# An MoE stage that is activated in place in PSUM, with its queues in written order

## The chip, the core and the metric

One core of a Trainium2 chip runs the whole program. The metric is device time in microseconds (us) of one execution. The core has five engines that this document speaks of: TensorE (PE) multiplies matrices into PSUM, eight banks of 512 fp32 columns on 128 partitions; VectorE (DVE) and ScalarE (ACT) read and write both PSUM and SBUF; GpSimd (POOL) works on SBUF alone; SyncE (SP) issues the DMAs. Each engine takes its instructions strictly in the order of its own queue, so an instruction that waits holds up all behind it.

## What is computed

Attention with a cluster mask over 2 x 8 heads, then two MoE-like layers on 1536 tokens of width 512 (2048 hidden). Only the two layers are touched:

```python
x = attn_out.transpose(0, 2, 1, 3).reshape(1536, 512)
h = x @ w_in;  g = maximum(0.01 * h, h);  x = g @ w_out        # layer one
h = x @ w2_in; r = maximum(h, 0); g = r * r; out = g @ w2_out   # layer two
```

Everything is fp32 in and out. TensorE gets each operand as a high and a low part in a reduced format (`xh`, `xl`, `wh`, `wl`, `gh`, `gl`), and each product is three matmuls: high by high, high by low, low by high.

## The kernel before

**Layers.** A layer is eight pairs of 128-wide slices f of the hidden dimension. Tokens are three blocks b of 512. A unit (`g1`) is h of one b and one f: four 128-deep chunks times three, 12 matmuls of 128x512 into one PSUM bank. It is activated (`act`) to `gh` and `gl` in SBUF; then `g2` multiplies them with the second weight, 12 matmuls over four banks `o`, which are open over the two f of a pair. After a pair, `flush` moves the four banks: into `acc` by ACT for the first pair (L839), added to it by DVE for the others (L842), and for the last pair added (L846), then split to `xh` (ACT, L847) and `xl` (DVE and POOL in turn, L848) as the next layer's input.

**Plain pairs and quads.** The first `PLAIN[m]` pairs of layer m are plain: six units. The others are quads: blocks 0 and 1 and both f are taken together by seven products in place of eight (`quad`), 42 matmuls in place of 48, and block 2 by two units. The quad needs sums of rows of x (`t_pieces`: `whole` at L896 on DVE joins high and low part, `minus` on POOL at L904, and `keep` splits the result into `th` on ACT and `tl` on DVE and POOL at L909), one overwritten part of x (`t_last`, L932 and L933), and a third weight block of sums (`sum_pieces`, POOL, L190). All of the x sums are written into the last plain pair, f = 2. Block 2's two `g2` stand in the next pair ("behind").

**Weights.** A slice's weight block is loaded as 8-byte floats (1 MB, `wraw`, one buffer, L140, SP queue) and made fp32: `mag` on ACT (L149), `shift`, `low`, `sign` on DVE (L153, L159, L166), then split: `wh` on ACT (L128), `wl` on POOL (L129). The next load can start only when `sign` has read the raw words. The pieces are laid evenly between the steps of the pair before.

**Activation.** Layer one: ACT applies Prelu twice to the bank, once to `gh`, once to an SBUF tile `g` (L795, L796), and `gl` is their difference (L803), on DVE for units, on POOL inside a quad. Layer two: ACT writes Relu to an SBUF tile `t` (L799), DVE squares it to `g` (L800), ACT rounds to `gh` (L801), then `gl`. Inside a quad the pieces are first added from a bank and an SBUF tile to another SBUF tile `q` (L871, L884, L888).

**What sets the order.** The attention stage is written out by hand. From `manual.close()` (L718), near attention's end, a planner that works with estimated durations orders PE, DVE, ACT and POOL; it takes the `ps_h` pool's four banks in turn and mixes matmuls of several units. SP's queue is in written order, and so is PE's last step.

Of the kernel before, what the change touches and what calls it, by code (L numbers as in the profile page):

```python
# [52 lines left out]
def attention_moe_moe_kernel(  # L53
# [69 lines left out]
    def split_block(ci, t):  # L123
        pool = next(q for q, n in ring if ci % RING < n)
        wh = pool.tile([128, 2 * DM], F32R, tag="wh", name="wh")
        wl = pool.tile([128, 2 * DM], F32R, tag="wl", name="wl")
        weights[blocks[ci]] = (wh, wl)
        nc.scalar.copy(out=wh, in_=t)  # L128
        nc.gpsimd.tensor_tensor(out=wl, in0=t, in1=wh.bitcast(F32), op=ALU.subtract)  # L129

    def decode_pieces(ci):

# [35 lines left out]
                op0=ALU.bitwise_and, op1=ALU.bitwise_or,  # L168
            )

        def split():
            split_block(ci, st["t"].bitcast(F32))

        return [load, mag, shift, low, sign, split]

    def sum_pieces(ci):

        st = {}
        K = DM // 2

        def sums():
            w = st["w"] = stg[1].tile([128, 4, K], F32, tag="ws", name="ws")
            t0, t1 = words.pop(ci - 2), words.pop(ci - 1)
            for o, i, k, op in (
                (w[:, 0], t1[:, 0:K], t1[:, K : 2 * K], ALU.add),
                (w[:, 1], w[:, 0], t0[:, 0:K], ALU.subtract),
                (w[:, 2], t0[:, 0:K], t1[:, 0:K], ALU.subtract),
                (w[:, 3], t0[:, K : 2 * K], w[:, 1], ALU.subtract),
            ):
                nc.gpsimd.tensor_tensor(out=o, in0=i, in1=k, op=op)  # L190

        def split():
            split_block(ci, st["w"].rearrange("p a b -> p (a b)"))

        return [sums, split]

    def pool_copy(out, in_):
        nc.gpsimd.tensor_scalar(
# [574 lines left out]
    def x_in(kk, b):  # L773
        return tuple(x[:, kk, b * N : (b + 1) * N] for x in (xh, xl))
# [61 lines left out]
    def flush(m, b, g, o, ps):  # L836
# [19 lines left out]

    def quad(m, f, between):
# [6 lines left out]
        U = ps_h.tile([128, N], F32, tag="h", name="h")  # L864
        p(U, lambda k: w_in(f0, k), lambda k: x_in(k, 0), True)
        p1 = tmp()
        nc.scalar.copy(out=p1, in_=U)
        V = ps_h.tile([128, N], F32, tag="h", name="h")
        p(V, lambda k: w_in(f0, 2 + k), lambda k: x_in(2 + k, 0), True)
        h = tmp()  # L870
        nc.vector.tensor_tensor(out=h, in0=V, in1=p1, op=ALU.add)  # L871
        act(m, 0, f, h, True)
        between(0)
        p(U, lambda k: w_in(s, 2 + k), lambda k: t_in(1, k), False)
        u2 = tmp()
        nc.scalar.copy(out=u2, in_=U)
        W = ps_h.tile([128, N], F32, tag="h", name="h")
        p(W, lambda k: w_in(s, k), lambda k: t_in(0, k), True)
        p5 = tmp()
        nc.scalar.copy(out=p5, in_=W)  # L880
        between(1)
        p(U, lambda k: w_in(s, 4 + k), lambda k: t_in(2, k), False)
        h = tmp()
        nc.vector.tensor_tensor(out=h, in0=U, in1=p5, op=ALU.add)  # L884
        act(m, 1, f + 1, h, True)
        p(W, lambda k: w_in(s, 6 + k), lambda k: x_in(2 + k, 1), False)
        h = tmp()
        nc.vector.tensor_tensor(out=h, in0=W, in1=u2, op=ALU.add)  # L888
        act(m, 1, f, h, True)
        p(U, lambda k: w_in(f1, 2 + k), lambda k: t_in(3, k), False)  # L890
        act(m, 0, f + 1, U)

    def whole(k, b):
        h, l = x_in(k, b)
# [2 lines left out]
        return t  # L897

    def t_pieces(kk):
        st = {}  # L900

        def minus(x, y, *tag):
            t = tmp(*tag)
            nc.gpsimd.tensor_tensor(out=t, in0=x, in1=y, op=ALU.subtract)  # L904
            return t

        def keep(i, t):
            nc.scalar.copy(out=th[:, i, kk], in_=t)
            (nc.vector if i % 2 else nc.gpsimd).tensor_tensor(  # L909
                out=tl[:, i, kk], in0=t, in1=th[:, i, kk].bitcast(F32), op=ALU.subtract  # L910
            )

        def first():
            st["b12"] = whole(kk, 1)
            st["t"] = minus(st["b12"], whole(kk, 0))
            keep(0, st["t"])

        def second():
            st["b22"] = whole(2 + kk, 1)
            st["t"] = minus(st["b22"], st["t"])  # L920
            keep(1, st["t"])

        def third():
            keep(2, minus(st["b22"], st["b12"]))
            t_late[kk] = minus(whole(2 + kk, 0), st["t"], "t4", 2)

        return [first, second, third]
# [9 lines left out]
    def step_list(m, f, prev):  # L937
# [9 lines left out]
        if f < 2 * PLAIN[m]:  # L947
# [5 lines left out]
            if f == 2 * PLAIN[m] - 2:  # L953
                t = t_pieces(0) + t_pieces(1)
                seq = [g for p in zip(seq, t) for g in p] + seq[len(t) :]
                seq += [lambda: (t_last(0), t_last(1))]
# [12 lines left out]
    for m in range(2):
        for f in range(0, NF, 2):  # L970
            seq, prev = step_list(m, f, prev)
            after = (m, f + 2) if f + 2 < NF else (m + 1, 0)
            pcs = []
            for i, block in enumerate(blocks):
                if block[:2] == after:
                    pcs += (sum_pieces if block[2] == 2 else decode_pieces)(i)
            done = 0
            for i, step in enumerate(seq):
                if (m, f, i) == (1, NF - 2, len(seq) - 1):
                    with tc.manual_schedule(engines={mybir.EngineType.PE}):  # L980
                        step()
                else:
                    step()
                if (m, f, i) == (0, 0, 0):
                    for pc in decode_pieces(1):
                        pc()
                upto = len(pcs) * (i + 1) // len(seq)
                for pc in pcs[done:upto]:
                    pc()
                done = upto  # L990
# [47 lines left out]
```

## Time and profile before

| | us |
|---|---|
| median of the runs (3: 793.75 to 794.24) | 794.1 |
| the profiled execution | 793.11 |
| its span, first to last instruction | 791.3 |
| PE busy in the span | 758.3 |
| DVE busy | 619.5 |
| POOL busy | 451.8 |
| ACT busy | 443.9 |

A stretch is read from the busy time of PE, the number of its instructions and the granted clock there. An instruction's row gives its start, its duration, what it makes of what, and, in brackets, how long its engine had been idle before it and who released it. PE's matmuls overlap, so the pace is read from starts, not from durations.

### The profile page before, as it was taken

The numbers are of one execution on the slowest core, as the hardware profiler recorded it, in microseconds if no ns is written. First come the engines' busy times: TensorE is split into PE (matmuls) and PEld (weight loads), VectorE is DVE, ScalarE is ACT, GpSimd is POOL, SyncE is SP. The second block draws the span as 40 slices with busy tenths as digits, with TensorE's granted clock in tenths as the row PEclk, the third lists the DMA queues.
The fourth block names the chain that finished last, engine by engine and source line by source line (L and its number), as shares of the span: only waits on it lengthen the run. The fifth ranks groups of instructions, "written<-read, shape, count | busy, mean of one in ns | idle before, by whom it ended". The sixth has DMA issues, their size and how long they took to land.

```text
span 791.3 us, 11086 instructions
## 1 busy us (share of the span) xinstructions
PE 758.3 (96%) x4075; PEld 655.6 (83%) x4075; DVE 619.5 (78%) x838; ACT 443.9 (56%) x823; POOL 451.8 (57%) x372
## 2 busy tenths in 40 slices
PE   8899999999999898989999999989799999999998
PEld 8899999999988776868887888866588888888886
DVE  5899999999998987664776773899787687877654
ACT  6988988988997455344253452545443444344420
POOL 2989889888863874445354441687543435273410
PEclk9999999999999998999999999999999999999999
DMA  7584474463403122320330221111311102111004
GB/s 221 121 204 108 111 170 118 109 154 92 123 1 108 54 80 80 106 88 20 106 107 1 77 86 51 53 54 54 101 60 59 48 22 86 54 54 53 1 1 159
DMA packets 16006, 66.35 MB, mean 84 GB/s; under 512 B 2704, under 2 KB 2704, under 8 KB 10960
## 3 DMA queue, kind: packets, MB, share of 16 engines
q1 hardware_dynamic: 15952, 65.64, 28.2%
q8 instruction: 32, 0.52, 0.3%
q14 instruction: 22, 0.18, 0.1%
HBM read 44.60 MB, written 3.15 MB: 60 GB/s over the span
## 4 chain that ended last, share of the span: by engine, by line
PE 62%; DVE 24%; ACT 6%; issue 3%; DMA 3%; POOL 2%; DVEq 0%; ACTq 0%; POOLq 0%; SPq 0%
PE o L826 26%; PE h L764 21%; PE S L386 4%; PE A L484 4%; DVE el L466 4%; PE T L449 4%; DVE nm L409 4%; DMA wraw<-w 3%; DVE q L896 2%; ACT e L419 2%; DVE wt L159 2%; DVE wt L166 2%; DVE gl L803 2%; DVE wt L153 2%; POOL ws L190 1%
## 5 line engine op out<-in xcount | busy, mean ns | idle before, releaser
L842 DVE TENSOR_TENSOR acc<-o,acc 128x512 f32<-128x512 f32 x144 | 95.0, 685 | 51.8 <-PE o L826 51.7
L803 POOL TENSOR_TENSOR gl<-g,gh 128x512 fp32r<-128x512 f32 x36 | 52.4, 1462 | 125.7 <-ACT gh L801 71.2
L129 POOL TENSOR_TENSOR wl<-wt,wh 128x1024 fp32r<-128x1024 f32 x32 | 81.1, 2535 | 61.4 <-ACT wh L128 61.2
L764 PE MATMUL h<-xl,wh 128*128 128x512 f32 x288 | 112.4, 390 | 0.6 <-DVE xl L848 0.6
L764 PE MATMUL h<-xh,wh 128*128 128x512 f32 x288 | 112.0, 391 | 0.0
L764 PE MATMUL h<-xh,wl 128*128 128x512 f32 x288 | 110.8, 390 | 0.0
L436 POOL TENSOR_SCALAR e<-e,r 128x768 f32<-128x768 f32 x96 | 88.5, 932 | 21.5 <-DVE r L433 14.2
L466 DVE TENSOR_TENSOR el<-T,eh 128x512 fp32r<-128x512 f32 x144 | 94.3, 683 | 5.8 <-ACT eh L460 3.9
L409 DVE TENSOR_REDUCE nm<-S 128x1 f32<-128x768 f32 x96 | 90.7, 946 | 4.1 <-PE S L290 2.3
L419 ACT ACTIVATE e<-S,nm 128x768 f32<-128x768 f32 x96 | 87.0, 907 | 11.0 <-DVE nm L409 6.7
L386 PE MATMUL S<-hb 128*128 128x384 f32 (+1 forms) x384 | 90.6, 350 | 1.9 <-ACT e L419 1.2
L460 ACT CAST eh<-T 128x512 fp32r<-128x512 f32 x144 | 79.4, 586 | 11.9 <-PE T L449 11.4
L826 PE MATMUL o<-wh,gh 128*128 128x512 f32 x192 | 76.6, 399 | 8.0 <-ACT acc L839 5.3
L484 PE MATMUL A<-eh,vv 128*128 128x256 f32 x288 | 79.5, 306 | 2.6 <-DVE xt L506 2.6
L449 PE MATMUL T<-ident,e 128*128 128x128 f32 x576 | 79.7, 274 | 1.2 <-DVE el L466 1.0
L826 PE MATMUL o<-gl,wh 128*128 128x512 f32 x192 | 76.7, 399 | 3.8 <-DVE gl L803 3.8
L826 PE MATMUL o<-gh,wh 128*128 128x512 f32 x192 | 73.1, 399 | 6.1 <-ACT acc L839 3.1
L826 PE MATMUL o<-wl,gh 128*128 128x512 f32 x192 | 75.8, 395 | 0.0
L826 PE MATMUL o<-gh,wl 128*128 128x512 f32 x192 | 75.7, 396 | 0.0
L826 PE MATMUL o<-wh,gl 128*128 128x512 f32 x192 | 73.1, 396 | 1.8 <-DVE gl L803 1.8
L484 PE MATMUL A<-el,vv 128*128 128x256 f32 x288 | 72.5, 282 | 0.3 <-DVE el L466 0.3
L449 PEld LDWEIGHTS T<-ident,e 128*128 128x128 f32 x576 | 68.3, 144 | 5.2 <-POOL e L436 1.7
(136 smaller groups left out, 1694.3 us busy)
## 6 DMA issues: line engine op xcount, KB each, us to landing
wraw<-w SPq DMA_DIRECT2D x32, 1024.0 KB, 4.7
hb<-spl SPq DMA_DIRECT2D x14, 576.0 KB, 4.7
hb<-spl SPq DMA_DIRECT2D x42, 192.0 KB, 4.9
rqk<-qk SPq DMA_DIRECT2D x16, 384.0 KB, 4.2
rv<-v SPq DMA_DIRECT2D x8, 384.0 KB, 4.0
out<-q SPq DMA_DIRECT2D x12, 256.0 KB, 2.0
twice<-qk SPq DMA_DIRECT2D x8, 192.0 KB, 5.9
hb<-st SPq DMA_DIRECT2D x28, 48.0 KB, 2.6
```

Of the source, the lines that this page charges most:

```text
L129: nc.gpsimd.tensor_tensor(out=wl, in0=t, in1=wh.bitcast(F32), op=ALU.subtract)
L386: nc.tensor.matmul(out=s[:, c, 0:HALF], lhsT=hb[0:k, a, i * 128 : (i + 1) * 128], rhs=hb[0:k, b, c * HALF : (c + 1) * HALF], start=(a == 0 ...
L409: nc.vector.tensor_reduce(out=n, in_=s_t[t][:, :, 0:HALF], axis=AX.XY, op=ALU.max, negate=True)
L419: nc.scalar.activation(out=e.rearrange("p (a b) -> p a b", a=2), in_=s_t.pop(t)[:, :, 0:HALF], func=AF.Exp, bias=n_t.pop(t), scale=1.0, ac ...
L436: nc.gpsimd.tensor_scalar(out=e_t[t], in0=e_t[t], scalar1=r_t[t // 2][:, t % 2 : t % 2 + 1], scalar2=1.0, op0=ALU.mult, op1=ALU.mult,)
L449: nc.tensor.transpose(T[:, o : o + 128], e_t[2 * u + b][:, kc * 128 : (kc + 1) * 128], ident)
L460: nc.scalar.copy(out=eh[:, 2 * g : 2 * g + 2, :].rearrange("p a b -> p (a b)"), in_=T_t[u, g])
L466: nc.vector.tensor_tensor(out=el[:, 2 * g : 2 * g + 2, :].rearrange("p a b -> p (a b)"), in0=T_t.pop((u, g)), in1=eh[:, 2 * g : 2 * g + 2, ...
L484: nc.tensor.matmul(out=A, lhsT=w, rhs=m[:, kc, :], start=(kc == 0 and i == 0), stop=(kc == KC - 1 and i == 1),)
L764: nc.tensor.matmul(out=out, lhsT=l, rhs=r, start=(first and i == 0), stop=(i == n - 1), skip_group_check=not first,)
L826: nc.tensor.matmul(out=outs[o], lhsT=l, rhs=r, start=(first and i == 0), stop=(last and i == 2),)
L842: nc.vector.tensor_tensor(out=a, in0=ps, in1=a, op=ALU.add)
```

## The change

In layer one the first three pairs are plain (two before); layer two keeps two. `act` works in the unit's own bank: the second Prelu, the square and the quad's three additions write back to PSUM, the square as max(h, 0) times Relu's tile in one DVE instruction, and `gl` is always DVE's, also in quads. The four `ps_h` banks are taken by name: U, V, W, X in a quad, fixed ones for units. The steps of a quad become three (`first`, `second`, `third`), and inside `third` the activation's parts of three units are interleaved by hand. From the second pair of layer one, (m, f) = (0, 2), to the end PE, DVE, ACT and POOL run in written order; the first pair stays with the planner. A table `TURN` says after which step of a pair each piece of the next pair's weights stands (0 load, 1 mag, 2 shift, 3 low, 4 sign, 5 `wh`, 6 `wl`; block 2: sums, `wh`, `wl`; block "3" is the load for the pair after next). The x sums are cut into eight pieces a chunk, one after each step from `SUMS`, so over pairs two and three of layer one and over the first two pairs of layer two; `minus` and all of `tl` and `xl` are POOL's, `whole` stays DVE's.

```diff
-    PLAIN = (2, 2)
+    PLAIN = (3, 2)
...
-        nc.gpsimd.tensor_tensor(out=wl, in0=t, in1=wh.bitcast(F32), op=ALU.subtract)
+        return lambda: nc.gpsimd.tensor_tensor(
+            out=wl, in0=t, in1=wh.bitcast(F32), op=ALU.subtract
+        )
...
-    ps_h = ctx.enter_context(tc.tile_pool(name="ps_h", bufs=4, space=PSUM, reuse_waits="tile"))
+    ps_h = ctx.enter_context(tc.tile_pool(name="ps_h", bufs=1, space=PSUM, reuse_waits="tile"))
...
-        h = ps_h.tile([128, N], F32, tag="h", name="h")
+        h = bank((2 * b + f + f // 2 * 2) % 4 if f < 2 * PLAIN[m] else (1, 3)[f % 2])
...
+        def relu():
             nc.scalar.activation(out=t, in_=h, func=AF.Relu)
-            nc.vector.tensor_tensor(out=g, in0=t, in1=t, op=ALU.mult)
-            nc.scalar.copy(out=gh, in_=g)
-        eng = nc.gpsimd if inside else nc.vector
-        eng.tensor_tensor(out=gl, in0=g, in1=gh.bitcast(F32), op=ALU.subtract)
-        parts[m, b, f] = gh, gl
+
+        def square():
+            nc.vector.scalar_tensor_tensor(
+                out=h, in0=h, scalar=0.0, in1=t, op0=ALU.max, op1=ALU.mult
+            )
+
+        def high():
+            if m == 0:
+                nc.scalar.activation(out=gh, in_=h, func=AF.Prelu, alpha=0.01)
+                nc.scalar.activation(out=h, in_=h, func=AF.Prelu, alpha=0.01)
+            else:
+                nc.scalar.copy(out=gh, in_=h)
+
+        def low():
+            nc.vector.tensor_tensor(out=gl, in0=h, in1=gh.bitcast(F32), op=ALU.subtract)
+            parts[m, b, f] = gh, gl
...
-            (nc.vector if o % 2 else nc.gpsimd).tensor_tensor(
+            nc.gpsimd.tensor_tensor(
                 out=xl[:, o, c], in0=a, in1=xh[:, o, c].bitcast(F32), op=ALU.subtract
             )
...
+        U, V, W, X = (bank(i) for i in range(4))
+
+        def first():
+            p(U, lambda k: w_in(f0, k), lambda k: x_in(k, 0), True)
+            p1 = tmp()
+            nc.scalar.copy(out=p1, in_=U)
+            p(V, lambda k: w_in(f0, 2 + k), lambda k: x_in(2 + k, 0), True)
+            add(V, V, p1)
+            act(m, 0, f, V)
...
+        def third():
+            u2, p5 = kept
+            p(U, lambda k: w_in(s, 4 + k), lambda k: t_in(2, k), False)
+            add(X, U, p5)
+            x = acts(m, 1, f + 1, X)
+            w = acts(m, 1, f, W)
+            u = acts(m, 0, f + 1, U)
...
+        return [
+            lambda: (whole("b12", kk, 1), whole("b11", kk, 0)),
+            lambda: (minus("t1", "b12", "b11"), whole("b22", 2 + kk, 1)),
+            lambda: (minus("t2", "b22", "t1"), high(0, "t1")),
+            lambda: (low(0, "t1"), high(1, "t2")),
+            lambda: (minus("t3", "b22", "b12"), whole("b21", 2 + kk, 0)),
+            lambda: (low(1, "t2"), high(2, "t3")),
+            lambda: (minus("t4", "b21", "t2", "t4", 2), t_late.update({kk: st["t4"]})),
+            lambda: low(2, "t3"),
+        ]
...
-            lambda: quad(m, f, lambda i: i < len(behind) and behind[i]()),
+            first, behind[0], second, behind[1], third,
             out_of(0, 0), unit(2, 0), out_of(0, 1), unit(2, 1), out_of(1, 0), out_of(1, 1),
...
+    TURN = (
+        ((0, 1),), ((0, 2), (0, 3)), ((0, 4), (1, 0)), ((0, 5),), ((0, 6), (1, 1)),
+        ((1, 2), (1, 3)), ((1, 4), (2, 0)), ((1, 5), (1, 6), (3, 0)), ((2, 1),), ((2, 2),),
+    )
+    SUMS = ((11, 22), (3, 11))
+    LAST = (30, 19)
```

ACT at the end of attention, where layer one's first pair begins (`T` and `A` are attention's banks, `h_3736` is the first unit's bank, `wh` and `wt` the weight block for the second pair), before:

```order
L497 COPY xt_3483<-A_3654 64x256
L460 CAST eh_3660<-T_3681 128x512
L149 ACTIVATE wt_3788<-wraw_3767 128x1024
L497 COPY xt_3483<-A_3687 64x256
L795 ACTIVATE gh_3750<-h_3736 128x512
L796 ACTIVATE g_3749<-h_3736 128x512
L795 ACTIVATE gh_3783<-h_3769 128x512
L796 ACTIVATE g_3782<-h_3769 128x512
L128 CAST wh_3847<-wt_3788 128x1024
```

and with the change:

```order
L151 ACTIVATE wt_3768<-wraw_3766 128x1024
L499 COPY xt_3483<-A_3654 64x256
L462 CAST eh_3660<-T_3681 128x512
L128 CAST wh_3827<-wt_3768 128x1024
L499 COPY xt_3483<-A_3687 64x256
L811 ACTIVATE gh_3749<-h_3736 128x512
L812 ACTIVATE h_3736<-h_3736 128x512
L811 ACTIVATE gh_3783<-h_3770 128x512
```

The weight block's `wh` now stands ahead of attention's last copy and of the first unit's activation; it stood behind both. On PE the second unit and part of two others moved ahead of attention's last product `A_3687`, and right behind that product stand now the first `g2`'s matmuls.

DVE in layer two's first pair (`q` from `xh`,`xl` are the x sums, `acc` from `o` is the flush of layer one), before:

```order
L848 TENSOR_TENSOR xl_67<-acc_3733,xh_66 128x512
L800 TENSOR_TENSOR g_5773<-t_5776 128x512
L153 TENSOR_SCALAR wt_6019<-wt_6019 128x1024
L896 TENSOR_TENSOR q_6075<-xh_66,xl_67 128x512
L846 TENSOR_TENSOR acc_3733<-o_5726,acc_3733 128x512
L159 SCALAR_TENSOR_TENSOR wt_6019<-wraw_6001,wt_6019 128x1024
L800 TENSOR_TENSOR g_5796<-t_5799 128x512
L803 TENSOR_TENSOR gl_5775<-g_5773,gh_5774 128x512
L909 TENSOR_TENSOR tl_3735<-q_6023,th_3734 128x512
L896 TENSOR_TENSOR q_6077<-xh_66,xl_67 128x512
L848 TENSOR_TENSOR xl_67<-acc_3733,xh_66 128x512
```

and with the change:

```order
L866 TENSOR_TENSOR acc_3733<-o_5664,acc_3733 128x512
L805 SCALAR_TENSOR_TENSOR h_5692<-h_5692,t_5707 128x512
L817 TENSOR_TENSOR gl_5706<-h_5692,gh_5705 128x512
L805 SCALAR_TENSOR_TENSOR h_5714<-h_5714,t_5729 128x512
L817 TENSOR_TENSOR gl_5728<-h_5714,gh_5727 128x512
L155 TENSOR_SCALAR wt_5712<-wt_5712 128x1024
L161 SCALAR_TENSOR_TENSOR wt_5712<-wraw_5592,wt_5712 128x1024
L805 SCALAR_TENSOR_TENSOR h_5736<-h_5736,t_5751 128x512
L817 TENSOR_TENSOR gl_5750<-h_5736,gh_5749 128x512
L168 SCALAR_TENSOR_TENSOR wt_5712<-wraw_5592,wt_5712 128x1024
L959 TENSOR_TENSOR q_5778<-xh_66,xl_67 128x512
L959 TENSOR_TENSOR q_5780<-xh_66,xl_67 128x512
```

The flush ends before the layer's first unit, `xl` is gone from DVE, and the x sums come in twos and ones behind the units' activations.

## Rows read from the trace of the kernel before

**Rows 1.** The page's first line: span and instructions

```profile
span 791.3 us, 11086 instructions
```

**Rows 2.** Stretches: length; PE, PEld, DVE, ACT, POOL busy us (instructions); PE clock; DMA share, GB/s

```profile
269.98:310.86 40.88, 33.94 (x129) 26.66 (x128) 34.24 (x25) 21.61 (x37) 27.37 (x17) 0.87 0.21 77
...
340.32:351.50 11.18, 8.47 (x37) 6.68 (x36) 5.63 (x8) 6.38 (x12) 2.58 (x2) 1.00 0.24 94
...
524.00:571.00 47.00, 36.75 (x140) 27.68 (x139) 42.09 (x36) 22.35 (x37) 33.45 (x21) 0.93 0.16 52
...
588.00:787.67 199.67, 199.63 (x881) 164.91 (x879) 141.88 (x183) 75.14 (x116) 73.68 (x48) 1.00 0.14 51
```

**Rows 3.** PE's waits from 240 us on: for whom, total us, times, longest

```profile
PE o L826 <- ACT acc L839: 8.4, 3, 3.1
PE o L826 <- DVE gl L803: 5.6, 3, 3.3
PE o L826 <- ACT gh L795: 2.7, 1, 2.7
...
PE A L484 <- DVE xt L506: 0.5, 1, 0.5
```

**Rows 4.** DVE in order of time, 276 to 283 us: start, us, instruction

```profile
276.08 1.28 DVE L896 TENSOR_TENSOR q<-xh,xl 128x512 f32<-128x512 f32 x2
277.28 2.37 DVE L803 TENSOR_TENSOR gl<-g,gh 128x512 fp32r<-128x512 f32 x2
279.58 3.47 DVE L896 TENSOR_TENSOR q<-xh,xl 128x512 f32<-128x512 f32 x2
```

**Rows 5.** ACT in order of time at two of PE's waits; idle, releaser in brackets

```profile
298.70 1.12 ACT L149 ACTIVATE wt<-wraw 128x1024 f32<-128x1024 f32 x1 [2.82 <-DMA wraw<-w]
299.72 2.04 ACT L839 COPY acc<-o 128x512 f32<-128x512 f32 x4
...
347.43 1.12 ACT L149 ACTIVATE wt<-wraw 128x1024 f32<-128x1024 f32 x1 [3.17 <-DMA wraw<-w]
```

**Rows 6.** Groups by line and shape from 240 us: busy us, mean ns, idle before

```profile
L842 DVE TENSOR_TENSOR acc<-o,acc 128x512 f32<-128x512 f32 x144 | 95.0, 685 | 51.8 <-PE o L826 51.7
L803 DVE TENSOR_TENSOR gl<-g,gh 128x512 fp32r<-128x512 f32 x60 | 59.0, 998 | 16.2 <-ACT g L796 12.0 <-ACT gh L801 3.8
L800 DVE TENSOR_TENSOR g<-t 128x512 f32<-128x512 f32 x48 | 52.4, 1103 | 12.2 <-ACT t L799 12.0
...
L801 ACT CAST gh<-g 128x512 fp32r<-128x512 f32 x48 | 29.7, 620 | 47.8 <-DVE g L800 47.8
...
L904 POOL TENSOR_TENSOR q<-q 128x512 f32<-128x512 f32 x12 | 20.4, 1716 | 11.5 <-DVE q L896 11.5
```

**Rows 7.** DVE's decoding while POOL is idle (348 us) and busy (286 us)

```profile
348.58 0.69 DVE L153 TENSOR_SCALAR wt<-wt 128x1024 int32<-128x1024 int32 x1 [5.51 <-ACT wt L149]
349.31 1.23 DVE L159 SCALAR_TENSOR_TENSOR wt<-wraw,wt 128x1024 int32<-128x1024 int32 x1
...
286.38 1.77 DVE L153 TENSOR_SCALAR wt<-wt 128x1024 int32<-128x1024 int32 x1
288.19 2.20 DVE L159 SCALAR_TENSOR_TENSOR wt<-wraw,wt 128x1024 int32<-128x1024 int32 x1
```

**Rows 8.** Layer one's start in order of time: two matmuls of PE, two steps of ACT

```profile
241.95 0.47 PE L764 MATMUL h<-xh,wh 128*128 128x512 f32 x1
...
255.44 0.40 PE L764 MATMUL h<-xh,wl 128*128 128x512 f32 x1
...
253.52 1.14 ACT L149 ACTIVATE wt<-wraw 128x1024 f32<-128x1024 f32 x1 [1.70 <-DMA wraw<-w]
...
260.33 1.05 ACT L128 CAST wh<-wt 128x1024 fp32r<-128x1024 f32 x1 [1.31 <-DVE wt L166]
```

**Rows 9.** The page's DMA part: the weight load's row, KB each, us to landing

```profile
wraw<-w SPq DMA_DIRECT2D x32, 1024.0 KB, 4.7
```

**Rows 10.** The chain that ended last, its last stretch on PE: start, us, what

```profile
774.03 13.61 PE o L826 x60
```

More of the change, by code (lines that the diff above doesn't have):

```diff
@@ L169, in sign @@
             )
-        def split():
-            split_block(ci, st["t"].bitcast(F32))
-        return [load, mag, shift, low, sign, split]
+        def high():
+            st["rest"] = split_block(ci, st["t"].bitcast(F32))
+        return [load, mag, shift, low, sign, high, lambda: st["rest"]()]
     def sum_pieces(ci):
@@ L873, in quad @@
[L873 to L884, printed above, removed]
@@ new lines, in quad, with second @@
+        kept = []
+        def second():
+            for q, i, o, fresh in ((U, 2, 1, False), (W, 0, 0, True)):
+                p(q, lambda k: w_in(s, i + k), lambda k: t_in(o, k), fresh)
+                kept.append(tmp())
+                nc.scalar.copy(out=kept[-1], in_=q)
+        def third():
[5 more added lines that the diff above has]
+            u = acts(m, 0, f + 1, U)
+            if m:
+                x.pop(0)()
+            p(W, lambda k: w_in(s, 6 + k), lambda k: x_in(2 + k, 1), False)
+            if m:
+                x.pop(0)()
+            x.pop(0)()
+            add(W, W, u2)
+            if m:
+                w.pop(0)()
+            p(U, lambda k: w_in(f1, 2 + k), lambda k: t_in(3, k), False)
+            if m:
+                u.pop(0)()
+            x.pop(0)()
+            for q in (w, u):
+                if m:
+                    q.pop(0)()
+                q.pop(0)()
+            w.pop(0)()
+            u.pop(0)()
@@ L893, in whole @@
+        return first, second, third
     def whole(k, b):
@@ L900, in t_pieces, with minus, high, low @@
         st = {}
[L902 to L910, printed above, removed]
-            )
[L913 to L927, printed above, removed]
+        def minus(out, x, y, *tag):
+            st[out] = tmp(*tag)
+            nc.gpsimd.tensor_tensor(out=st[out], in0=st[x], in1=st[y], op=ALU.subtract)
+        def high(i, t):
+            nc.scalar.copy(out=th[:, i, kk], in_=st[t])
+        def low(i, t):
+            nc.gpsimd.tensor_tensor(
+                out=tl[:, i, kk], in0=st[t], in1=th[:, i, kk].bitcast(F32), op=ALU.subtract
+            )
+        def whole(out, k, b):
+            h, l = x_in(k, b)
+            st[out] = tmp()
+            nc.vector.tensor_tensor(
+                out=st[out], in0=h.bitcast(F32), in1=l.bitcast(F32), op=ALU.add
+            )
[9 more added lines that the diff above has]
+        ]
     def t_last(kk):
@@ L952, in step_list @@
             seq += [unit(1, 0), out_of(0, 0), unit(1, 1), out_of(0, 1)]
[L953 to L956, printed above, removed]
             seq += [unit(2, 0), out_of(1, 0), unit(2, 1), out_of(1, 1)]
             return seq, tail
+        first, second, third = quad(m, f)
         seq = [
-            lambda: quad(m, f, lambda i: i < len(behind) and behind[i]()),
+            first, behind[0], second, behind[1], third,
             out_of(0, 0), unit(2, 0), out_of(0, 1), unit(2, 1), out_of(1, 0), out_of(1, 1),
@@ L966, in step_list, with piece @@
         return seq, tail
+    TURN = (
+        ((0, 1),), ((0, 2), (0, 3)), ((0, 4), (1, 0)), ((0, 5),), ((0, 6), (1, 1)),
+        ((1, 2), (1, 3)), ((1, 4), (2, 0)), ((1, 5), (1, 6), (3, 0)), ((2, 1),), ((2, 2),),
+    )
+    SUMS = ((11, 22), (3, 11))
+    LAST = (30, 19)
+    order = ctx.enter_context(ExitStack())
+    pieces = {}
+    def piece(block, j):
+        if block not in blocks:
+            return
+        if block not in pieces:
+            i = blocks.index(block)
+            pieces[block] = (sum_pieces if block[2] == 2 else decode_pieces)(i)
+        pieces[block][j]()
@@ L968, in attention_moe_moe_kernel, with pair_after @@
+    def pair_after(m, f):
+        return (m, f + 2) if f + 2 < NF else (m + 1, 0)
     prev = []
     for m in range(2):
-        for f in range(0, NF, 2):
-            seq, prev = step_list(m, f, prev)
[L972 to L977, printed above, removed]
-            for i, step in enumerate(seq):
[L979 to L983, printed above, removed]
-                if (m, f, i) == (0, 0, 0):
[L985 to L990, printed above, removed]
+        turn = 0
+        sums = {}
+        for kk in range(2):
+            for i, t in enumerate(t_pieces(kk)):
+                sums.setdefault(SUMS[m][kk] + i, []).append(t)
+            sums.setdefault(LAST[m] + kk, []).append(lambda kk=kk: t_last(kk))
+        for f in range(0, NF, 2):
+            if (m, f) == (0, 2):
+                order.enter_context(
+                    tc.manual_schedule(
+                        engines={
+                            mybir.EngineType.PE,
+                            mybir.EngineType.DVE,
+                            mybir.EngineType.Activation,
+                            mybir.EngineType.Pool,
+                        }
+                    )
+                )
+            seq, prev = step_list(m, f, prev)
+            after = pair_after(m, f)
+            later = pair_after(*after)
+            for i, step in enumerate(seq):
+                step()
+                if (m, f, i) == (0, 0, 0):
+                    for j in range(7):
+                        piece((0, 0, 1), j)
+                    piece((0, 2, 0), 0)
+                for k, j in TURN[i] if i < len(TURN) else ():
+                    piece((*later, 0) if k == 3 else (*after, k), j)
+                for t in sums.pop(turn, ()):
+                    t()
+                turn += 1
```

42 lines of the change are left out of this document (15 added, 27 removed).

## The prediction

> **What bounds the kernel now.** I read the chain that ended last first: it closes with 60 matmuls of PE without a break [rows 10]. So the question is where PE is off its pace in the MoE part. The stretch from 588 us to the last matmul shows the pace: 880 matmuls (one of the 881 began ahead of the edge) in 199.67 us, 0.227 each, PE never idle and its clock at 1.00 [rows 2]. A unit or a `g2` of 12 is then 2.72 us. Held against that pace, three stretches lose time: 269.98 to 310.86 has 128 matmuls, 29.0 us of work in 40.9, so 11.8 lost; 340.32 to 351.50 has 36, 8.2 in 11.2, 3.0 lost; 524 to 571 has 139, 31.5 in 47.0, 15.5 lost [rows 2]. Together 30.3 us; the rest of the MoE part is at the pace within half a us. Part of the first and the last is clock: 0.87 and 0.93 of full there, that is, matmuls at the lower of the clock's two levels behind a wait.
>
> Who makes PE wait is the next view: ACT's copy of the flush, `gl` from DVE, `gh` from ACT [rows 3]. The engines in order of time show two reasons. First, ACT stands at `mag`, whose load has not landed, 2.82 us at 296 and 3.17 at 344, and the copies and Prelus that PE wants are queued behind it [rows 5]. Secondly, DVE is full with x sums: `gl` at 277.28 takes 2.37 for two and stands between sums that take 1.28 and 3.47 [rows 4]; in the last stretch DVE is busy 42.1 of 47.0 us, POOL 33.5 [rows 2]. Both are matters of order and of place, not of total work.
>
> **What the change removes.** The x sums leave the two crowded places: eight pieces a chunk, one after each step of 2.72 us. DVE loses all its `tl` and `xl` parts but `t_last`. A stall such as that at 277 then has no sum in front of `gl`. The squares and `gl` get an operand from PSUM: they took 1103 and 998 ns with both inputs in SBUF, where the flush, one input in PSUM, takes 685 [rows 6]. In quads three `gl` come from POOL to DVE, 3 x 0.69 = 2.1 us, and the six squares and three old `gl` of layer two give back 6 x 0.42 + 3 x 0.31 = 3.4. DVE's queue in a quad of layer two is 27 such operations (12 flush, 6 square, 6 `gl`, 3 add), 18.5 us, and two decodings of some 3.2 with POOL idle, 25 of the 31.3 us of its 138 matmuls: no new bound. And in written order `mag` stands four steps behind its load for block 0 (10.9 us, landing takes 4.7 [rows 9]) and two for block 1 (5.4 in a plain pair, 6.8 in a quad), with the activation due first ahead of it. I take all 30.3 us as removed, and price what is late next:
>
> - The third plain pair: 48 matmuls in place of 42, 6 x 0.227 = **1.4**. Its block of sums that goes saves POOL and ACT work beside PE: nothing.
> - Layer one's first pair, still the planner's, but in another order. Before, PE gets from 241.95 to 255.44 through 25 unit matmuls and all of attention's rest [rows 8], 13.5 us, 0.5 of them a wait [rows 3]: attention's part is 13.5 - 0.5 - 5.7 = 7.3. Now 42 unit matmuls stand ahead of its last product, which ends at 241.95 + 9.5 + 7.3 = 258.8. Behind it comes the first `g2`, whose `gh` is queued on ACT behind `wh`. From the load's landing at 253.5 [rows 8]: `mag` 1.1, shift 0.7, two attention steps on DVE 1.0, low and sign 1.2 each [rows 7], `wh` 1.05 [rows 8], a copy 0.4, `gh` 0.6 [rows 6]: 7.2, so 260.7. PE waits 1.9, and 0.1 for `gl`: **2.0**. Ends: 0 if the load lands 2 us earlier; 4.7 if the clock falls behind the wait as it does in the first stretch, where 0.13 of 40.9 us, 5.3, went to two falls. I take no fall, since none follows the wait of 2.7 near 346 (clock 1.00 in that stretch [rows 2]).
> - The second pair of layer two: bank o0 must be flushed when out_of(1,0) begins, 9 steps in, at 24.5. Unit (0,1) ends at 8.2; Relu, square, round, `gl` about 2.9 with their hand-overs; sign 1.2; load 4.9 to 17.3; `mag` 1.1, shift 0.7, low 1.2, a `whole` 0.7, the square, round and `gl` of unit (1,1) 2.0, sign 1.2, flush 0.7: 25.0, 0.5 late. With POOL on the same side, shift, low and `whole` take about 1 us more each [rows 7], 3.4 late. POOL's seven sums of 1.72 [rows 6] and its splits fill about half that pair, so I take the middle, **2.0**.
> - Pairs two and three of layer one: the same chain without squares ends about 0.9 early, or 2.0 late with POOL beside it; **0.5** for both.
> - Quads of layer two, five with decoding: out_of(1,0) begins at 25.8; unit (2,0) ends at 20.4, then 0.2 of pipeline, Relu 0.6, square 0.7, round 0.6, `gl` 0.7, sign 1.2, flush 0.7 and hand-overs 0.3: 25.4, 0.4 early. Writing to PSUM by DVE is shown by no row; at the same 685 nothing, at twice that 0.3 late, 1.5 in all: **0.5**.
> - Layer two's start: POOL makes all twelve `xl`. Block 1's are ready by 4 x 1.72 = 6.9 us behind the flush, and its first unit stands 10.9 behind; block 2's by about 13.8, due at 21.8. Nothing, with 4 us of cover.
>
> **The sum**, against the profiled execution (span 791.3 [rows 1], 793.11 with what lies around it): 793.1 - 30.3 + 1.4 + 2.0 + 2.0 + 0.5 + 0.5 = 769.2. The median of the runs is 1.0 above that execution; so 770.2. The end, 3.7 us from the last matmul's end at 774.03 + 13.61 [rows 10], stays.
>
> **Rivals.** (1) *DVE and POOL collide in the plain pairs.* All of `tl` is now POOL's, in a steady stream beside decoding. If each of shift, low, `whole`, sign meets a POOL instruction, at 1.1 extra each [rows 7], the chain grows by 4.4 - 0.5: late by 4.4 in layer two and 3.0 twice in layer one, 10.4 in place of 2.5: 778. For it: DVE's means for two SBUF inputs [rows 6]. Against: POOL is idle half the time. The Trainium skill, SBUF — State Buffer (SBUF: two separate sides), says that the pair of ports that DVE and POOL share is locked for a whole instruction. By that rule the four would each wait for a POOL instruction of 1.72, 6.9 us a pair, and the time would be 787; the rows, 1.0 to 1.1 extra, show about two thirds of that.
>
> (2) *The in-place writes are slow.* At twice 685 ns the additions and squares make `gl` of the last unit of `third` late for out_of(0,1) by 0.2, besides the 0.3 above: 0.5 in eleven quads, 5.5 for 0.5, so 775.
>
> (3) *The change does not reach where most is lost.* The first pair stays with the planner. If the 11.8 us of the first stretch stay: 770.2 + 11.8 - 2.0 = 780. Against: half of that stretch is pair two's, and the sums leave pair one.
>
> (4) *Slower: ACT in written order stands at a `mag` that has not landed, in every pair.* A wait such as that at 344 costs PE 2.7 [rows 3]; in fifteen pairs 40, so 811. It decides from (794.1 - 770.2) / 15 = 1.6 us a pair. For it: block 1's load waits for sign, which stands behind a unit's `gl`. Against: the two steps and more between load and `mag`, and behind `mag` on ACT the next work is due only after another 2.7 us.
>
> **How the numbers follow.** The forecast, 765 to 775, has 0.65; (1) 0.13, (2) 0.07, (3) 0.08, (4) 0.07, of which 0.05 slower and 0.02 about even, where it strikes in part of the pairs. The low end has all small terms at nothing, 793.1 - 30.3 + 1.4 + 1.0 = 765.2, and 0.7 less for the small waits that I left in. The high end takes in (1) to (3): 780. Beyond 0.2% (1.6 us, about what a measurement of this kernel can tell from no change) faster has 0.93, within it 0.02, slower 0.05.
>
> **What would show it.** In the changed profile: no PE wait over 2.5 us from 240 us on, PE's clock at 1.00 from there to the end, no `mag` with idle for its load followed by a PE wait, squares and `gl` near 0.69 us. One PE wait of about 2 us for `gh` near 259 us, and waits for the flush, under 4 us, in layer two's second pair. I am wrong if the quads show a wait each, if in-place instructions take over 0.9 us, or if the waits moved to layer two's first pair.

## The result, and the profile after

The changed kernel takes 770.4 us (median of four runs, 769.35 to 770.78) against 793.9 for the kernel before: ratio 0.970, 95% interval 0.9686 to 0.972. The forecast was 770.2. The profiled execution took 770.16 us. Its page, the span and the share of each engine (busy us, share of the span, instructions), against [rows 1]:

```profile
span 768.4 us, 11090 instructions
PE 751.3 (98%) x4081; PEld 653.5 (85%) x4081; DVE 569.5 (74%) x861; ACT 444.1 (58%) x819; POOL 384.6 (50%) x341
```

Busy time by stretch from the first flush group on (length; PE, weight load, DVE, ACT, POOL busy with instructions; granted clock; DMA share; GB/s), the view of [rows 2]:

```profile
254.00:270.00 16.00, 13.29 (x56) 10.59 (x55) 9.12 (x11) 6.74 (x12) 5.02 (x3) 0.89 0.25 74
270.00:520.00 250.00, 250.00 (x1104) 207.01 (x1103) 157.02 (x205) 114.73 (x179) 97.91 (x66) 1.00 0.18 63
520.00:565.00 45.00, 42.16 (x183) 33.95 (x183) 29.94 (x38) 24.68 (x40) 23.59 (x18) 1.00 0.24 80
565.00:764.50 199.50, 199.50 (x881) 164.96 (x879) 146.16 (x205) 81.95 (x121) 59.84 (x41) 1.00 0.18 62
```

Two stretches of 250 and 199.5 us have PE busy in every us at clock 1.00; all eleven quads lie in them. What remains lost is in two short places, and the list of what PE waited for from 240 us on (waited for; us, times, longest) is short against [rows 3]:

```profile
PE o L846 <- ACT gh L811: 2.7, 1, 2.7
PE o L846 <- DVE acc L862: 1.7, 1, 1.7
PE o L846 <- ACT acc L859: 1.2, 2, 0.7
```

(The third row stands for two waits, 0.70 and 0.48.) The groups that answer to [rows 6] (busy us, mean ns; idle before):

```profile
L862 DVE TENSOR_TENSOR acc<-o,acc 128x512 f32<-128x512 f32 x144 | 92.6, 684 | 12.1 <-PE o L846 12.1
L817 DVE TENSOR_TENSOR gl<-h,gh 128x512 fp32r<-128x512 f32 x96 | 65.8, 690 | 76.8 <-ACT h L812 56.3 <-ACT gh L814 19.6
L805 DVE SCALAR_TENSOR_TENSOR h<-h,t 128x512 f32<-128x512 f32 x48 | 32.9, 696 | 25.0 <-ACT t L802 25.0
L151 ACT ACTIVATE wt<-wraw 128x1024 f32<-128x1024 f32 x31 | 35.0, 1129 | 9.7 <-DMA wraw<-w 7.8 <-POOL q L946 1.9
```

The squares, which write back into their PSUM bank, take 696 ns where they took 1103 from SBUF, `gl` 690 in place of 998. An in-place write costs what the flush (684) does. Of these 288 squares, `gl` and flushes 129 start while GpSimd is at work, and none takes over 0.70 us.

The largest loss left is at layer one's start. ScalarE in order of time (start, us, what, idle before it and its releaser), then PE:

```profile
258.86 1.04 ACT L128 CAST wh<-wt 128x1024 fp32r<-128x1024 f32 x1 [3.33 <-DVE wt L168]
259.93 0.36 ACT L499 COPY xt<-A 64x256 f32<-64x256 f32 x1
260.32 0.60 ACT L811 ACTIVATE gh<-h 128x512 fp32r<-128x512 f32 x1
...
526.05 1.14 ACT L151 ACTIVATE wt<-wraw 128x1024 f32<-128x1024 f32 x1 [1.89 <-POOL q L946]
527.09 2.03 ACT L859 COPY acc<-o 128x512 f32<-128x512 f32 x4
```

```profile
260.97 1.19 PE L846 MATMUL o<-gh,wh 128*128 128x512 f32 x4 [2.69 <-ACT gh L811]
262.18 0.63 PE L846 MATMUL o<-gl,wh 128*128 128x512 f32 x1
262.61 0.63 PE L846 MATMUL o<-gh,wl 128*128 128x512 f32 x1
```

`gh` is queued behind `wh`, which waits for sign: PE stands for 2.69 us, and behind that its matmuls start 0.43 us apart up to 265.6, the lower of the clock's two levels, another 2.0 us. The last two rows of ScalarE are layer two's first pair: `mag` of the second block stands 1.89 us and starts at 526.05, and the accumulator copies for which PE waits (0.70) are queued behind it. The row names a sum of POOL that ends then, but the block's load, issued at 521.29, lands within 0.1 us of it (4.7 us, as in [rows 9]), and in experiment 7 the row of the same `mag` names the load:

```profile
522.75 1.13 ACT L151 ACTIVATE wt<-wraw 128x1024 f32<-128x1024 f32 x1 [2.07 <-DMA wraw<-w]
```

### The profile page after: what moved, and what is told of

It reads as the page before. It is cut to its first block, busy times and chain, and to the rows that moved or that the text cites. A ratio compares the mean times of both kernels' runs of the same rounds, so it can differ in the third digit from the quotient of the medians.

```text
span 768.4 us, 11090 instructions
## 1 busy us (share of the span) xinstructions
PE 751.3 (98%) x4081; PEld 653.5 (85%) x4081; DVE 569.5 (74%) x861; ACT 444.1 (58%) x819; POOL 384.6 (50%) x341
## 4 chain that ended last, share of the span: by engine, by line
PE 74%; DVE 14%; ACT 8%; issue 1%; DMA 1%; POOL 1%; DVEq 0%; ACTq 0%; SPq 0%; POOLq 0%
PE o L846 31%; PE h L769 27%; PE A L486 4%; PE S L388 4%; DVE el L468 4%; PE T L451 4%; DVE nm L411 3%; ACT e L421 2%; DMA wraw<-w 1%; ACT eh L462 1%; DVE wt L168 1%; ACT wt L151 1%; DVE xt L508 1%; ACT acc L859 1%; PE warm L237 1%
## 5 line engine op out<-in xcount | busy, mean ns | idle before, releaser
L129 POOL TENSOR_TENSOR wl<-wt,wh 128x1024 fp32r<-128x1024 f32 x32 | 76.9, 2405 | 132.6 <-ACT wh L128 132.6
L817 DVE TENSOR_TENSOR gl<-h,gh 128x512 fp32r<-128x512 f32 x96 | 65.8, 690 | 76.8 <-ACT h L812 56.3
L769 PE MATMUL h<-xl,wh 128*128 128x512 f32 x296 | 115.2, 389 | 0.0
L769 PE MATMUL h<-xh,wh 128*128 128x512 f32 x296 | 115.2, 390 | 0.0
L769 PE MATMUL h<-xh,wl 128*128 128x512 f32 x296 | 115.1, 389 | 0.0
L862 DVE TENSOR_TENSOR acc<-o,acc 128x512 f32<-128x512 f32 x144 | 92.6, 684 | 12.1 <-PE o L846 12.1
L846 PE MATMUL o<-wh,gh 128*128 128x512 f32 x192 | 75.0, 391 | 2.8 <-DVE acc L862 1.7
L846 PE MATMUL o<-wh,gl 128*128 128x512 f32 x192 | 74.7, 389 | 0.0
```

The source lines that it names most:

```text
L129: return lambda: nc.gpsimd.tensor_tensor(out=wl, in0=t, in1=wh.bitcast(F32), op=ALU.subtract)
L769: nc.tensor.matmul(out=out, lhsT=l, rhs=r, start=(first and i == 0), stop=(i == n - 1), skip_group_check=not first,)
L846: nc.tensor.matmul(out=outs[o], lhsT=l, rhs=r, start=(first and i == 0), stop=(last and i == 2),)
```

## Experiments

Ratios are to the kernel before on the same chip (795 to 796 us there), so they compare where microseconds do not quite; the changed kernel run once more gave 0.9691 (0.9671 to 0.9712).

> The changed kernel once more, beside the three that are compared with it: ratio 0.970 to the kernel before, whatever the chip.

Theory W: the gain is the written order, which no longer lets an engine stand at work that is not ready while PE's work is queued behind. Rival P: the gain is PSUM as the place of the activations.

**1. Only the in-place results of the activation undone.** A quad's additions still write to PSUM, and `t` has two buffers in place of three (no Relu of this run waits for one).

```diff
-        t = tmp("t", 3) if m else None
+        t = tmp("t", 2) if m else None
+        g = tmp("g", 2)
...
-            nc.vector.scalar_tensor_tensor(
-                out=h, in0=h, scalar=0.0, in1=t, op0=ALU.max, op1=ALU.mult
-            )
+            nc.vector.tensor_tensor(out=g, in0=t, in1=t, op=ALU.mult)
...
-                nc.scalar.activation(out=h, in_=h, func=AF.Prelu, alpha=0.01)
+                nc.scalar.activation(out=g, in_=h, func=AF.Prelu, alpha=0.01)
...
-                nc.scalar.copy(out=gh, in_=h)
+                nc.scalar.copy(out=gh, in_=g)
...
-            nc.vector.tensor_tensor(out=gl, in0=h, in1=gh.bitcast(F32), op=ALU.subtract)
+            nc.vector.tensor_tensor(out=gl, in0=g, in1=gh.bitcast(F32), op=ALU.subtract)
```

> The changed kernel with the activations' results in SBUF tiles again (only the in-place writes undone; written order, sums on GpSimd and three plain pairs kept). Theory W, that the gain is the written order (ScalarE no longer stands at a mag whose load has not landed): 770 to 774 us; gl and square, 0.69 us each in the trace of the changed kernel, go up to 0.9 to 1.1 us each where GpSimd works beside them, and PE's new waits are some 0.5 to 2 us in the plain pairs of layer two alone. Rival P, that keeping DVE's operands in PSUM away from GpSimd is the gain: at least half of the 23.5 us comes back, 782 us or more, with PE waiting for gl in the quads too.

Measured: 780.3 us, ratio 0.981 (0.9788 to 0.9832), between the two: 1.1% or some 8.5 us come back, a third of the gain. The groups and the waits of PE:

```profile
L816 DVE TENSOR_TENSOR gl<-g,gh 128x512 fp32r<-128x512 f32 x96 | 90.2, 946 | 74.1 <-ACT g L811 52.2 <-ACT gh L813 20.6
L806 DVE TENSOR_TENSOR g<-t 128x512 f32<-128x512 f32 x48 | 42.3, 891 | 22.9 <-ACT t L803 22.9
```

```profile
PE o L845 <- DVE acc L861: 5.3, 2, 3.9
PE o L845 <- ACT acc L858: 4.1, 2, 2.3
PE o L845 <- ACT gh L810: 2.5, 1, 2.5
PE h L769 <- DVE h L884: 0.5, 1, 0.5
```

The durations are those that W named, and all the new waits but the 0.5 lie in layer two's plain pairs or right behind them. What W had too small is what a single collision costs. DVE and POOL of this run in layer two's first pair:

```profile
538.01 2.49 DVE L806 TENSOR_TENSOR g<-t 128x512 f32<-128x512 f32 x1 [1.01 <-ACT t L803]
541.18 0.99 DVE L816 TENSOR_TENSOR gl<-g,gh 128x512 fp32r<-128x512 f32 x1 [0.68 <-ACT gh L813]
```

```profile
537.56 2.39 POOL L129 TENSOR_TENSOR wl<-wt,wh 128x1024 fp32r<-128x1024 f32 x1 [4.22 <-ACT wh L128]
539.91 1.72 POOL L945 TENSOR_TENSOR q<-q 128x512 f32<-128x512 f32 x1
```

The square, 0.68 us alone, starts 0.45 behind `wl` and ends at 540.50, 0.55 behind `wl`'s end at 539.95: it stood until POOL was through. The same square of the changed kernel, DVE and then POOL:

```profile
534.97 0.70 DVE L805 SCALAR_TENSOR_TENSOR h<-h,t 128x512 f32<-128x512 f32 x1 [1.02 <-ACT t L802]
```

```profile
534.52 2.40 POOL L129 TENSOR_TENSOR wl<-wt,wh 128x1024 fp32r<-128x1024 f32 x1 [3.50 <-ACT wh L128]
```

It runs inside `wl`, and takes 0.70: with one of its two inputs in PSUM it does not wait. This holds for the whole run. In experiment 1, 38 of the 144 squares and `gl` start inside a GpSimd instruction, and all 31 that take over 0.72 us end 0.54 to 0.56 behind the end of one; the longest are the `gl` of layer two's quads:

```profile
609.31 2.82 DVE L816 TENSOR_TENSOR gl<-g,gh 128x512 fp32r<-128x512 f32 x1 [0.69 <-ACT gh L813]
```

In the changed kernel the same number start inside a GpSimd instruction, and none is longer than 0.70, also not a `gl`, which writes to SBUF.

**2. Only the written order taken off**, the planner ordering the four engines again.

```diff
             if (m, f) == (0, 2):
-                order.enter_context(
-                    tc.manual_schedule(
-                        engines={
-                            mybir.EngineType.PE,
-                            mybir.EngineType.DVE,
-                            mybir.EngineType.Activation,
-                            mybir.EngineType.Pool,
-                        }
-                    )
-                )
+                pass
```

> The changed kernel with the written order taken off (the planner orders the four engines of MoE as in the kernel before); in-place PSUM, sums on GpSimd and three plain pairs stay. Theory W: ScalarE's waits in front of mag for its load come back in the plain pairs, and PE loses 5 to 15 us there: 775 to 786 us. Rival P: 770 to 772 us, PE loses no more than now after 270 us of the span.

Measured: 785.8 us, ratio 0.988 (0.9858 to 0.9902): 1.8%, some 14 us, come back. W's size, but not at W's place. ScalarE's idle time in front of `mag` for its load is 18.7 us where the changed kernel has 7.8, and yet PE's list is headed by DVE:

```profile
PE o L846 <- DVE gl L817: 5.8, 2, 4.3
PE o L846 <- ACT gh L814: 4.2, 1, 4.2
PE o L846 <- ACT gh L811: 3.2, 2, 2.6
```

DVE in front of the end of the wait of 4.3, at 284.4:

```profile
272.36 4.60 DVE L959 TENSOR_TENSOR q<-xh,xl 128x512 f32<-128x512 f32 x2
278.44 1.46 DVE L155 TENSOR_SCALAR wt<-wt 128x1024 int32<-128x1024 int32 x1 [1.47 <-ACT wt L151]
279.82 1.75 DVE L959 TENSOR_TENSOR q<-xh,xl 128x512 f32<-128x512 f32 x1
281.50 2.28 DVE L161 SCALAR_TENSOR_TENSOR wt<-wraw,wt 128x1024 int32<-128x1024 int32 x1
283.70 1.27 DVE L817 TENSOR_TENSOR gl<-h,gh 128x512 fp32r<-128x512 f32 x2
```

Sums and decoding, stretched to 1.5 to 2.3 us each beside a busy POOL, stand in front of two `gl` of 0.64. The wait of 4.2 for `gh`, up to 535.60, has mostly the same cause: the square ahead of that `gh` starts at 533.47, 6.1 us behind the end of its Relu, with sums, decoding and flush ahead of it on DVE. So the written order gains above all by what stands ahead of square and `gl` on DVE; of the prediction's two reasons it is the second, [rows 4], more than the first, [rows 5].

The ratios of 1 and 2 are 1.1% and 1.8% above that of the changed kernel, 2.9% together; the whole change is 3.0%. That does not make them shares of the gain: experiment 6, which undoes a third part, takes back another 0.7%, so the three come to 3.6%. The parts overlap, and no run undoes two of them together.

**3. The written order with `mag` of the second block one step earlier**, in front of activations due before its load lands.

```diff
-        ((0, 1),), ((0, 2), (0, 3)), ((0, 4), (1, 0)), ((0, 5),), ((0, 6), (1, 1)),
+        ((0, 1),), ((0, 2), (0, 3)), ((0, 4), (1, 0)), ((0, 5), (1, 1)), ((0, 6),),
```

> The changed kernel with the second block's mag written one step earlier, in front of the activations of the step in which its load (4.8 us) lands. Theory W: ScalarE stands at mag some 2.5 us in each pair, idle until the DMA; in the five plain pairs PE then waits for gh or the accumulator copies, 2 to 8 us in sum, in the quads the slack of about 2.9 us hides it: 772 to 778 us. Rival: where ScalarE stands is of no weight (it is busy 58% of the span), 770 to 771 us.

Measured: 786.6 us, ratio 0.9892 (0.9865 to 0.9918), far over the 772 to 778. ScalarE's `mag` group, and two stretches with their granted clock:

```profile
L151 ACT ACTIVATE wt<-wraw 128x1024 f32<-128x1024 f32 x31 | 35.0, 1128 | 57.6 <-DMA wraw<-w 53.9 <-POOL q L946 3.7
```

```profile
529.00:540.00 11.00, 8.46 (x31) 6.54 (x31) 7.81 (x9) 7.05 (x12) 3.83 (x2) 0.84 0.01 1
...
566.00:580.00 14.00, 10.18 (x34) 7.92 (x33) 9.33 (x12) 5.29 (x8) 9.56 (x9) 0.76 0.21 76
```

Only the second block of a pair was moved, and at its `mag` ScalarE stands some 3.7 us (3.74 and 3.76 in layer two's first two pairs) where 2.5 was expected. The span is 16.4 us longer: 529 to 540 has 31 matmuls, 7.0 us of work, 4.0 lost; 566 to 580 has 34, 7.7, so 6.3 lost; two places of layer one, near 306 and 340, lose 1.9 and 0.7; five quads of layer two lose 1.0 to 1.5 us each. Besides the longer stand, the miss has two parts: the waits of 2.5 and 3.8 us in layer two's pairs were followed by the lower clock, which I had not priced, and the slack of 2.9 us, read in a quad of layer one, holds there (those quads lose nothing) but not in layer two, where square and round lie between Relu and `gl`. That an engine which is busy 58% of the span can cost 16 us by where it stands is shown.

**4. The kernel before with a third plain pair** (`PLAIN = (3, 2)` and nothing else), and **5. the changed kernel with two** (`PLAIN = (2, 2)`, `SUMS = ((3, 11), (3, 11))`, `LAST = (19, 19)`).

> The kernel before with a third plain pair in layer one and nothing else of the change. Theory W: PE does 1.4 us more work, the stretch of the first quad that lost 3.0 us may lose less, the stretches of 270 to 311 and 524 to 571 us stay as they are: 791 to 796 us. Rival, that the third plain pair is what made room and so the gain: under 788 us.

> The changed kernel with two plain pairs in layer one and x's sums in the first two pairs, as in the kernel before. PE has 6 matmuls less, 1.4 us. Theory: the sums now fall into the planner's pair and pair two, beside decoding, and DVE's flush and gl are late there as in the second pair of layer two (1.8 us): 1 to 4 us over the changed kernel. Rival, that room is not the point: 1.4 us under it.

Measured: 797.3 us, ratio 1.0027 (1.0011 to 1.0044), so about 2 us more in the kernel before, a little over the range expected; and 771.2 us, ratio 0.9692 (0.967 to 0.9714), no difference from the changed kernel. In the second, the 1.4 us of PE's work that go are paid for near 263 and 277, where PE now waits for `gl` (0.63) and for `gh` (0.25) as well. The third pair is not the gain, and in the changed kernel it is no cost. The collision that I expected of the sums in the planner's pair is small.

**6. Every second low part of x and of the sums on DVE**, as before the change.

```diff
-            nc.gpsimd.tensor_tensor(
+            (nc.vector if o % 2 else nc.gpsimd).tensor_tensor(
                 out=xl[:, o, c], ...
```

(the same for `tl`)

> The changed kernel with every second low part of x and of the sums (xl, tl) on VectorE, as in the kernel before. Theory S, that the place of the sums matters in layer two's plain pairs, where VectorE is late by 1.8 us already: 6 tl of 0.7 to 1.7 us each go in front of gl or flush, 2 to 6 us over the changed kernel. Rival, that in written order the sums fit anywhere: within 1 us of it.

Measured: 775.3 us, ratio 0.9758 (0.9738 to 0.9778): 5.0 us over the changed kernel on the same chip, the size that theory S had. PE waits 1.45 and 0.24 for the last additions of layer one, a place that S did not name (an `xl` of 1.28 stands behind every second of them on DVE); in the pairs that S named, 1.72 for copies near 530 and 2.28 for the flush near 565, 1.0 and 0.6 more than in the changed kernel.

**7. ScalarE in written order from layer one's first pair on.**

```diff
+            if (m, f) == (0, 0):
+                for j in range(7):
+                    piece((0, 0, 1), j)
+                act_order = tc.manual_schedule(engines={mybir.EngineType.Activation})
+                act_order.__enter__()
             if (m, f) == (0, 2):
+                act_order.__exit__(None, None, None)
                 order.enter_context(
...
-                    for j in range(7):
-                        piece((0, 0, 1), j)
```

> The changed kernel with ScalarE alone in written order from layer one's first pair on, so that gh of the first unit stands ahead of the wh that waited for sign (idle 3.33 us in the trace of the changed kernel). Theory C, that the clock fell because PE stood 2.69 us for gh: gh can start when attention's last copy is done, near 258.5 in place of 260.3, PE waits 0.5 to 1.2 us, TensorE's clock stays at 1.00, and the time is 3 to 4 us under that of the changed kernel. Rival, that the fall belongs to the end of attention and comes whatever the wait: 1.5 to 2 us under it, with clock 0.89 still in the stretch 254 to 270.

Measured: 766.9 us (766.18 to 768.1), ratio 0.9652 (0.9631 to 0.9673), 3.45 us under the changed kernel beside it (770.3). ScalarE, PE, and the stretch with its clock:

```profile
257.96 0.36 ACT L499 COPY xt<-A 64x256 f32<-64x256 f32 x1 [4.73 <-PE A L486]
258.35 0.60 ACT L811 ACTIVATE gh<-h 128x512 fp32r<-128x512 f32 x1
```

```profile
259.00 1.20 PE L846 MATMUL o<-gh,wh 128*128 128x512 f32 x4 [1.08 <-ACT gh L811]
```

```profile
254.00:270.00 16.00, 14.92 (x72) 12.41 (x71) 7.13 (x8) 6.57 (x12) 4.42 (x3) 1.00 0.20 67
```

`gh` starts right behind attention's last copy, PE waits 1.08 in place of 2.69, and the clock stays: 1.6 + 2.0. Theory C holds, and this is the fastest of the versions.

**8. Layer two's pairs rearranged as well**, on top of 7. The first version changes both plain pairs, the second the first pair alone, the third both, with `t_last` and the sums of decoded words later.

```diff
+    EASE = {
+        (1, 0): TURN[:4] + (((0, 6),), ((1, 1),), ((1, 2), (1, 3)), ((1, 4),), ((1, 5), (1, 6), (3, 0))),
+        (1, 2): TURN[:6] + ((), ((1, 4), (2, 0)), ((1, 5), (1, 6), (3, 0)), ((2, 1),), ((2, 2),)),
+    }
-    SUMS = ((11, 22), (3, 11))
+    SUMS = ((11, 22), (4, 12))
...
```

> As the run with ScalarE in written order from pair one on, and in layer two's first two pairs mag of the second block stands behind the accumulator copies, th of the third sum behind the second copies, and sign of the second pair's second block behind the flush; the sums start a step later. Theory: the losses of 0.86, 0.64 and 1.82 us at 526, 538 and 561 go, 2 to 3.3 us under that run, some 6 us under the changed kernel. Rival: a later mag only moves the lateness to wh of the next pair, so 0 to 1 us under that run.

> ScalarE in written order from pair one on, and the new order (mag behind the copies, sums one step later) in layer two's first pair alone, the second pair's table as in the changed kernel. The losses of 1.03 and 0.63 us at 523 and 535 go, the one of 1.83 at 558 stays: 1.2 to 1.7 us under the run with ScalarE alone, ratio near 0.963. Rival, that a mag behind the copies makes the second block's words late in pair two: no gain, 0 to 1 us over that run.

> As the run that changed both pairs of layer two, but with the second chunk's sums a further step later, the sums of decoded words behind wh, and t_last two steps later, so that t_last (2.5 us beside GpSimd) does not stand in front of the gl for which PE waited 2.18 us at 567. If that gl is what cost it: 2 to 3 us under that run, 762 to 765. If the flush is late whatever stands behind it (1.7 us at 556 there): within 1 us of the run with the first pair alone.

Measured: 769.3 us (ratio 0.9681), 769.4 (0.966, 0.9635 to 0.9685; its runs lie between 766.8 and 770.9) and 772.1 (0.9701). None is shown to beat 7: the second comes out as its rival had it, the other two miss both of their forecasts. In the profiled execution of the second, one of 766.9 us, the losses of 1.03 and 0.63 at 523 and 535 are gone as meant, and pair two's of 1.83 has grown to 3.43:

```profile
PE o L846 <- DVE acc L862: 3.3, 1, 3.3
```

```profile
536.85 0.62 ACT L949 CAST th<-q 128x512 fp32r<-128x512 f32 x1 [1.96 <-POOL q L946]
537.37 0.59 ACT L802 ACTIVATE t<-h 128x512 f32<-128x512 f32 x1
...
539.21 1.15 ACT L151 ACTIVATE wt<-wraw 128x1024 f32<-128x1024 f32 x1
```

PE comes to pair two's late flush 4.9 us earlier than in the changed kernel (556.16 for 561.05), but ScalarE stands 1.96 at `th`, as it did before (1.91), and the pair's first `mag` is only 3.3 earlier (539.21 for 542.52); the 1.6 between them is what the first pair had given. In the other two versions the flush is earlier (PE goes on at 557.66 and 558.56, where it was 559.82 in the second), so the order of pair two does matter there, but what was moved is paid for behind it: PE waits 2.2 and 4.8 us for a `gl` in the first quad. In the first version that `gl` and its square stand behind a `t_last` of 2.52; in the third the Relu that they need is queued on ScalarE behind the `wh` of the block of sums, which waits for POOL:

```profile
569.50 1.04 ACT L128 CAST wh<-ws 128x1024 fp32r<-128x1024 f32 x1 [4.87 <-POOL ws L192]
```

So the third version's question, whether `t_last` was the cause, stays open.

## Why the prediction was right

The total is right to 0.2 us, and part of that is luck: terms off by up to 2.7 us cancel. Three of the signs that were named failed: at layer one's start a wait of PE over 2.5 us (2.69) and a clock of 0.89, and in layer two's plain pairs a `mag` idle for its load (1.89 and 1.39 us) with a PE wait behind it.

- *The 30.3 us removed.* Right: nothing of the three stretches of [rows 2] is left but the priced ones. Small losses outside of them, the largest 0.6 and 0.3 us near 420 and 586, which the sum left in, 1.0 together, went as well. As for the causes, the prediction put "order" and "place" side by side without a share; undone alone, they cost 1.8% and 1.1%.
- *Attention's rest.* The sum left it as it was. From the first unit's start (241.95 in both) to the end of attention's last product, less the unit matmuls, PE took 8.0 us before and 6.8 now (42 unit matmuls, 9.5 us, and this row), with two waits of 0.55 and 0.19 gone. These 1.2 us were not foreseen.

```profile
258.01 0.28 PE L486 MATMUL A<-el,vv 128*128 128x256 f32 x1
```

- *The third plain pair, 1.4.* Paid in matmuls, but without it the time is the same (experiment 5).
- *Layer one's first pair, 2.0.* The place and the mechanism are right (`gh` queued behind `wh`), the size is the term that failed: 2.69 + 2.0 = 4.7, the upper bound that was given. "I take no fall" was the wrong choice. `gh` ended at 260.9, forecast 260.7, but attention's last product at 258.3, forecast 258.8, so the wait is 0.7 longer; the other 2.0 is the clock.
- *The second pair of layer two, 2.0.* Measured 1.8, with the chain as written out: `mag` behind a load, shift at 1.47 beside POOL, sign, flush.
- *Pairs two and three of layer one and the quads of layer two, 0.5 each.* Both nothing.
- *Layer two's first pair.* The step that was missed: 1.5 us (0.86 and 0.64). I looked at block 1's and 2's `xl`, but not at what is queued ahead of the accumulator copies on ScalarE: a `mag` that can start only at 526.05, and a `th` that waits for POOL's sum. "What would make it wrong" had named that place, without a price.

With these sizes the sum is 793.1 - 30.3 - 1.0 - 1.2 + 1.4 + 4.7 + 1.8 + 1.5 = 770.0; the execution took 770.2.

Of the rivals, (2) is out: in-place writes cost 690 to 696 ns. (3) is out, (4) did not come, but experiment 3 shows that it lay one step away in the table: 16 of the 24 us from which it would decide. On (1) the prediction took rows of 1.0 to 1.1 us extra [rows 7] for two thirds of a rule. The Trainium skill, SBUF — State Buffer (SBUF: two separate sides), says that of a DVE instruction with two inputs in SBUF and a GpSimd instruction that reads SBUF, the one that starts first holds the shared ports for its whole length and the other stands. Experiment 1 agrees: what is paid is what is left of POOL's instruction, 1.8 us when the square comes 0.45 behind a `wl` of 2.39. The time did not come to 787 because squares and `gl` now read a bank, and because in written order decoding seldom meets POOL: low and sign, 1.23 us alone, take 1.29 and 1.26 on average.

## What to carry to other kernels

Where VectorE and GpSimd both work from SBUF, leave in PSUM what was computed there: an input there made squares and `gl` indifferent to GpSimd, 0.70 us, where with both inputs in SBUF it was up to 2.82. In an order written by hand, ask of each instruction that waits for a load or another engine what is queued behind it; one step of difference was worth 15 us here, where the whole change is worth 23.5. And price a wait of PE with the lower clock behind it as an upper end that does happen; removing 1.6 us of waiting brought 3.45.

## What the runs showed of the hardware that I had not expected

How long PE stood does not alone say whether the clock falls. Behind 2.69 us (changed kernel, 261) and 2.54 us (experiment 3, 532) the matmuls start 0.43 us apart for some 3 to 5 us. Behind 3.27 us, in the second version of experiment 8, they start 0.23 apart at once, as behind the 2.7 of [rows 3] in the kernel before; behind 2.18 us, in the first version (569), they come to 0.43 apart after five matmuls:

```profile
559.82 0.47 PE L846 MATMUL o<-wh,gh 128*128 128x512 f32 x1 [3.27 <-DVE acc L862]
560.13 0.40 PE L846 MATMUL o<-wl,gh 128*128 128x512 f32 x1
560.36 0.39 PE L846 MATMUL o<-wh,gl 128*128 128x512 f32 x1
```

Ahead of the waits of 2.54 and 3.27 alike PE had run without a wait for over 180 us (since 341 and 272), so how long it worked before does not tell them apart either. The same program can go either way: the five executions of that second version took 766.8, 766.9, 769.4, 769.8 and 770.9 us, with a granted clock over the span of 1.000, 1.000, 0.998, 0.998 and 0.995, and the profiled one is of the first two. That it is this wait behind which the clock fell in the other three is likely, but not shown; what decides it stays open.
